# Linear attention with sparse experts on one core: first loads, last tile and last expert step rearranged

## The chip, the cores and the metric

One of the eight cores of a Trainium2 chip runs the whole program. The metric is device microseconds of one execution, the median over repeated runs. TensorE (PE) multiplies, VectorE (DVE), ScalarE (ACT) and GpSimd (POOL) do the elementwise work, and SyncE (SP) issues nearly all transfers and the transposes of activations. Each engine takes its instructions in the order in which the program lists them; an instruction that waits for a semaphore holds everything behind it on the same engine.

## The reference

Two layers, each of an attention part (A) and an expert part (B), on x of 2048 rows by 512, in bf16:

```python
def _A_ref(x, wqkv, wo):                       # x: layer-normed
    qkv = (x @ wqkv) -> q, k, v                # 32 heads of 16
    pq, pk = phi(q), phi(k)                    # phi(t) = where(t > 0, t + 1, exp(t)) + 1e-6
    kv  = einsum("bhsd,bhse->bhde", pk, v);  z = pk summed over s
    o   = (pq @ kv) / (pq . z + 1e-6)
    return o @ wo
def _B_ref(x, w_r, w_gate, w_up, w_down):      # x: layer-normed
    r   = x @ w_r
    idx = the two rows with the largest r
    y   = (silu(x[idx] @ w_gate) * (x[idx] @ w_up)) @ w_down * sigmoid(r[idx])
    return x + (y added to rows idx, zero elsewhere)
x = x + _A_ref(_layernorm(x), ...); x = x + _B_ref(_layernorm(x), ...)    # twice
```

The expert part touches two rows only, but it needs the two largest router values over all 2048 rows first.

## The kernel before, in words

The 2048 rows are 16 tiles of 128. Weights and all activations stay in SBUF. One call of `linear_attention_moe` lays down some 950 operations through `op` (lines 61 to 85): engine, estimated duration, what is read and written, PSUM or SBUF slots. `Plan.order` (115 to 171) then picks, step by step, the operation that can start first by those estimates; ties go by a due time to which `WEIGHTS` (54) adds a hand-tuned offset per kind of operation (such as 'phi_raw0') or per operation number. The result is a fixed instruction list for each engine. Nothing is rearranged at run time, so both the weights and the estimates decide what stands behind what.

**First layer, front.** `dma`, `x_load` and `xt_load` (228 to 257) load x by tiles, a transposed copy xt of the first twelve tiles (so that their keys need no transpose on the chip), and the weights. Both halves of wk go through ScalarE's queue, all others through SyncE's; every row of xt is brought in pieces of 256 elements, 512 bytes. Meanwhile PE spins on zeros (`spin`, 838, ten products). `wk_center` (857) subtracts the column mean from the key weights (wkc, two halves on DVE), `row_sums` (847) gives the row means of tiles 0 and 1 (nmr). `K_raw` (448) multiplies xt by wk for tiles 0 and 1, with a correction by a rank-one product of nmr and nwb, and by wkc for tiles 2 to 11; `phi_raw` (424) turns this into pk, two ACT operations and two of DVE (em, pk). `pre` (874) takes statistics of x on DVE (358), the scale on ACT (`rstd`, 370), the normalised tile xn on the engine that KIND1 (870) names, and its transpose through SyncE's queue (`trans`, 400). `G` (470) accumulates xn^T pk over all tiles in four PSUM banks. After the sixteen transposes SyncE issues the loads of wv, wot, wo, wd and wgu; `center` (790) needs wv.

**Rest of layer one.** `Q` (481), `kv` (501), `kw_one` (558), `den` (575) and `O` (609) give the queries, the folded weights KW, the denominators and the update of x. `mid_chain` (730) normalises the new x for the expert part and for layer two at once; K and G of layer two run while the expert step of layer one (1078 to 1206) goes on as a serial chain of small operations. Its result is patched into layer two's sums (1223 to 1300) before layer two's `kv`.

**Layer two, end.** `O(1, t)` writes the last x. The last tile is split into columns 0 to 256, 256 to 384 and 384 to 512 (623), all three in one PSUM bank; DVE adds each part, ACT squares it. `lin` (678) gives the router values. `topk` (970) is run on tiles 0 to 11 early and on all later; `gather_rows` (1379) selects the chosen rows by products with a one-hot column. Then come `gate_up` (1053), SiLU, the up product, and the down product with the direct term (1474 to 1486), the copy yo (1494) and the transfer of the two rows (1498). Beside this, `last_out` (1328) writes the other rows: OUTK (1345) names the engine of each tile, OUTG (1346) an event after which it may run, `store` (1341) sends four tiles at a time. The transfer of the two rows waits for all four stores, since it overwrites rows of them. ACT loads another function table (1447) before the last SiLU, after its outputs.

## Time and profile before

| | |
|---|---|
| median of 9 runs | 158.44 us (157.97 to 158.88) |
| profiled execution | 158.34 us, span of the trace 156.5 us, granted clock 0.995 |
| PE products | 146.5 us busy, 94% of the span |
| DVE, ACT, POOL | 130.0, 111.8, 28.3 us busy |
| PE's share of the chain that ended last | 76%; DVE 9%, ACT 6% |
| transfers | 17.15 MB, of 24499 packets 17952 under 512 B |

The busy time of PE holds modelled ends of pipelined products; twenty-two of its products (the spin and the filler L1396) compute nothing. A line of the timeline has start, length, engine, line, operation, output and inputs, and in brackets the idle time before it with what ended it. The view by stretch has, after the length, the busy us of PE, PEld, DVE, ACT and POOL, then the granted clock, the share of the transfer engines and GB/s. A line of SyncE's waits has the total, the number and the longest.

### The profile page before, as it was taken

What the parts mean: (1) busy time and instruction counts of PE and PEld (TensorE: products, weight loads), DVE (VectorE), ACT (ScalarE), POOL (GpSimd) and SP (SyncE); (2) the same over time, 40 slices, a digit from 0 to 9 for tenths busy, and PEclk for the clock granted to TensorE, in tenths of its full rate; (3) what the DMA queues carried; (4) which work ended last, traced back from release to release, by engine and by line L of the source; (5) the groups of instructions that cost most, each with busy time, mean ns of one, the idle gap of its engine ahead of it and who ended that gap; (6) DMA issues with size and microseconds to landing.
All of it is one profiled execution on the core that took longest, in us unless ns stands there. A gap on an engine that the chain in (4) does not pass through costs nothing.

```text
span 156.5 us, 3882 instructions
## 1 busy us (share of the span) xinstructions
PE 146.5 (94%) x1360; PEld 74.4 (48%) x1380; DVE 130.0 (83%) x481; ACT 111.8 (71%) x272; POOL 28.3 (18%) x78
## 2 busy tenths in 40 slices
PE   6989999998999999999999999999999999998870
PEld 2424444443544444444545545575444455465660
DVE  1799999877799999999999989843488999999840
ACT  3379899654568787799978647702478998898930
POOL 7801055200000000110321000300420000643200
PEclk9999999999999999999999999999999999999998
DMA  4999947548998000033154530000000000040560
GB/s 129 348 361 279 259 101 71 103 101 280 428 453 345 6 4 0 0 71 65 42 101 101 101 67 6 0 4 0 0 4 0 4 0 0 4 136 2 178 227 2
DMA packets 24499, 17.15 MB, mean 110 GB/s; under 512 B 17952, under 2 KB 22560, under 8 KB 24096
## 3 DMA queue, kind: packets, MB, share of 16 engines
q1 hardware_dynamic: 24184, 16.39, 36.4%
q10 hardware_dynamic: 296, 0.53, 0.9%
q8 instruction: 10, 0.16, 0.4%
q14 instruction: 9, 0.07, 0.2%
HBM read 10.62 MB, written 2.10 MB: 81 GB/s over the span
## 4 chain that ended last, share of the span: by engine, by line
PE 76%; DVE 9%; ACT 6%; issue 4%; DMA 3%; SPq 0%; ACTq 0%; DVEq 0%
PE mm L487 18%; PE g L473 17%; PE g L618 11%; PE mm L441 9%; PE mm L454 5%; DVE x L628 4%; ACT pk L1334 3%; PE tp L843 3%; DMA wv<-in_A_wv_dram 3%; DVE pq L604 2%; PE tp L581 1%; PE tp L1059 1%; PE g L563 1%; PE mm L597 1%; PE tp L711 1%
## 5 line engine op out<-in xcount | busy, mean ns | idle before, releaser
L408 ACT ACTIVATE e<-mm 128x512 bf16<-128x512 f32 x52 | 30.4, 596 | 12.6 <-PE mm L441 6.3
L473 PE MATMUL g<-pk,xn 128*128 128x512 bf16 x123 | 31.1, 379 | 0.9 <-DVE pk L432 0.6
L487 PE MATMUL mm<-xnT,wq 128*128 128x512 bf16 x121 | 31.0, 379 | 0.6 <-issue 0.3
L618 PE MATMUL g<-KW,pq 128*128 128x512 bf16 (+2 forms) x134 | 30.3, 366 | 0.6 <-DVE x L628 0.4
L636 ACT ACTIVATE sq<-x 128x512 bf16<-128x512 bf16 (+2 forms) x34 | 20.4, 601 | 2.9 <-DVE x L628 2.5
L441 PE MATMUL mm<-wk,xnT 128*128 128x512 bf16 x76 | 19.5, 379 | 0.3 <-issue 0.2
L473 PEld LDWEIGHTS <-xn 128*128 128x128 bf16 x128 | 12.0, 98 | 15.8 <-issue 2.3
L618 PEld LDWEIGHTS <-pq 128*128 128x128 bf16 x136 | 12.6, 97 | 13.9 <-issue 0.5
L412 DVE TENSOR_SCALAR em<-e 128x512 bf16<-128x512 bf16 x52 | 15.1, 297 | 3.7 <-ACT e L408 3.5
L487 PEld LDWEIGHTS <-wq 128*128 128x128 bf16 x128 | 11.4, 97 | 12.5 <-issue 0.8
L394 POOL TENSOR_SCALAR xn<-x,s,nb 128x512 bf16<-128x512 bf16 x6 | 4.9, 822 | 52.5 <-PE g L618 37.5
L419 DVE SCALAR_TENSOR_TENSOR pk<-mm,em 128x512 bf16<-128x512 f32 x20 | 13.7, 687 | 0.3
L358 DVE BATCH_NORM_STATS2 st<-x 128x6 f32<-128x512 bf16 x16 | 10.5, 673 | 3.4 <-DMA x<-in_A_x_dram 3.4
L628 DVE SCALAR_TENSOR_TENSOR x<-x,opr,g 128x512 bf16<-128x512 bf16 (+2 forms) x18 | 11.9, 683 | 0.4 <-PE g L618 0.3
L441 PEld LDWEIGHTS <-xnT 128*128 128x128 bf16 x80 | 7.4, 98 | 8.8 <-DMA xnT<-xn 0.4
L628 DVE SCALAR_TENSOR_TENSOR x<-x,g 128x512 bf16<-128x512 bf16 x16 | 10.8, 683 | 0.7 <-PE g L618 0.5
L419 DVE SCALAR_TENSOR_TENSOR pq<-mm,em 128x512 bf16<-128x512 f32 x16 | 10.7, 685 | 0.1
L411 ACT ACTIVATE rl<-mm 128x512 bf16<-128x512 f32 x16 | 9.4, 612 | 1.8 <-DVE pq L416 1.0
L604 DVE TENSOR_TENSOR pq<-pq,rd 128x1024 bf16<-128x1024 bf16 x16 | 10.4, 685 | 0.0
L454 PE MATMUL mm<-wkc,xt 128*128 128x512 bf16 x39 | 10.1, 379 | 0.1
L427 ACT ACTIVATE e<-mm,rho 128x512 bf16<-128x512 f32 x12 | 8.2, 682 | 1.2 <-PE mm L460 1.2
L373 ACT ACTIVATE lnv<-mv,eps_t 128x2 f32<-128x2 f32 (+3 forms) x18 | 5.2, 291 | 5.1 <-DVE mv L359 3.5
(263 smaller groups left out, 232.0 us busy)
## 6 DMA issues: line engine op xcount, KB each, us to landing
wgu<-in_B_wgu_dram SPq DMA_DIRECT2D x2, 1408.0 KB, 13.7
out_dram<-pk SPq DMA_DIRECT2D x4, 512.0 KB, 3.9
wd<-in_B_wd_dram SPq DMA_DIRECT2D x1, 1408.0 KB
x<-in_A_x_dram SPq DMA_DIRECT2D x4, 256.0 KB, 5.4
xt<-in_A_xt_dram SPq DMA_DIRECT2D x4, 256.0 KB, 5.5
x<-in_A_x_dram SPq DMA_DIRECT2D x2, 512.0 KB, 5.9
wk<-in_A_wk_dram ACTq DMA_DIRECT2D x2, 256.0 KB, 4.0
wq<-in_A_wq_dram SPq DMA_DIRECT2D x1, 512.0 KB, 7.3
```

The source lines that it names most:

```text
L358: dve(0.61, lambda: V.bn_stats(out=st()[:], in_=x[:, t, :]), r=[("x", t)], w=[st]).early = 4.0
L408: act(0.5, lambda: A.activation(out=e()[:], in_=p()[:], func=ACT.Exp), r=[p], w=[e], **k)
L412: dve(0.2, lambda: V.tensor_scalar(out=em()[:], in0=e()[:], scalar1=1.0, scalar2=TINY, op0=ALU.min, op1=ALU.add), r=[e], w=[em], port=True ...
L419: dve(0.6, lambda: V.scalar_tensor_tensor(out=out_ap, in0=p()[:], scalar=0.0, in1=em()[:], op0=ALU.max, op1=ALU.add), r=[p, em], w=[key], **k)
L441: T_.matmul(p()[:], lhsT=xnT[:, c, t * P : (t + 1) * P], rhs=wk[:, c, :], start=(c == 0), stop=(c == NC - 1))
L454: T_.matmul(p()[:], lhsT=xt[:, c, t * P : (t + 1) * P], rhs=w[:, c, :], start=(c == 0), stop=(t >= NM and c == NC - 1),)
L473: T_.matmul(Gs[c]()[:], lhsT=xn[:, t, gcol(c) : gcol(c) + P], rhs=pk[:, t, :], start=first, stop=last)
L487: T_.matmul(p()[:], lhsT=wq[:, i, c, :], rhs=xnT[:, i, j * D : (j + 1) * D], start=(i == 0), stop=(i == NC - 1))
L604: dve(0.6, lambda q=q: V.tensor_tensor(out=q, in0=q, in1=rd()[:].to_broadcast([P, 2, D]), op=ALU.mult), r=[rd], w=[("pq", j, c), ("pq", j, ...
L618: T_.matmul(p()[:, a : a + n], lhsT=pqt(c, t * P, P), rhs=KWs[layer][:, c, a : a + n], start=(c == 0), stop=(c == NC - 1),)
L628: dve(0.04 + 0.6 * n / D, lambda q=q, a=a, n=n: V.scalar_tensor_tensor(out=x[:, t, a : a + n], in0=x[:, t, a : a + n], scalar=1.0 if i == ...
L636: act(0.1 + 0.5 * n / D, lambda q=q, a=a, n=n, sq=sq: A.activation(out=sq()[:, 0:n], in_=x[:, t, a : a + n], func=ACT.Square, scale=float( ...
```

## The change

The first half of wk and the first x load are issued by ScalarE, the second half of wk by SyncE, ahead of its other loads. xt is laid out by pairs of tiles, so that a row of a 256-column piece is 2 KB in one stretch. The order and the earliest times of the loads change (wq behind five transposes, xt 8 to 12 ahead of them). The estimate of the transfer rate in the planner goes from 284 to 355. Weights are named by kind and number within the kind, and all are new; KIND1, MIDK, OUTK, OUTG and the starts QA, QB, QD are new too, so the order of every engine's list changes. The three parts of the last tile each have a PSUM bank. The last gather goes to two banks, two column blocks each, and DVE adds each half by itself. Gate and up start with a product by zeros that clears their banks, in three banks (gate, first four and last seven blocks of up), and add first the two column blocks of the first gathered half, then the other two. Sigmoid of the router value is made with Exp before the table load instead of Tanh after it. The down products stand in two groups (blocks 0 to 3, 4 to 10). The twelve 512-wide fillers become 24 of 128.

```diff
-    WEIGHTS = {'phi_raw0': -3.7, 'kw_one0': 3.8, ...
+    WEIGHTS = {'phi_raw0': -8, 'den1': -8, 'mid_chain0': -7.8, ...
...
+        i = self.num[self.kind] = self.num.get(self.kind, -1) + 1
+        wt = self.WEIGHTS.get(self.kind, 0.0) + self.WEIGHTS.get(f"{self.kind}#{i}", 0.0)
...
-                bw = max(bw, o.done) + o.kb / 284.0
-                o.done = bw
+                bw = max(bw, o.done - 0.4) + o.kb / 355.0
+                o.done = bw + 0.8
...
-    xt = big.tile([P, NC, NR * P], BF16, name="xt")
+    xt = big.tile([P, NR // 2, NC, 2 * P], BF16, name="xt")
...
-    for k in range(0, NC, 2):
-        dma(wk[:, k : k + 2, :], A_wk[:, k : k + 2, :], [("wk", k)], 256, eng="ACT")
+    wk_load(0, eng="ACT", prio=-50.0)
+    x_load(0, 2, eng="ACT", prio=-49.0)
     op("ACT", 1.28, lambda: nc.scalar.preload_act_table_set("natural_log_exp_and_others"), w=["table"])
...
+    wk_load(2, prio=-50.0)
+    loads = [
+        (xt_load, 0, 2, 0.0), (x_load, 2, 4, 0.0), (xt_load, 2, 4, 0.0), (x_load, 4, 6, 0.0), (xt_load, 4, 6, 0.0),
+        (x_load, 6, 8, 3.5), (xt_load, 6, 8, 3.5), (x_load, 8, 12, 5.5),
+    ]
...
-    KIND1 = ['POOL', 'DVE', 'DVE', 'POOL', 'ACT', 'DVE', 'DVE', 'POOL', 'POOL', 'POOL', 'DVE', 'DVE', 'POOL', 'ACT', 'POOL', 'ACT']
-    QA, QT = 3, 8
+    KIND1 = ['POOL', 'ACT', 'POOL', 'DVE', 'DVE', 'ACT', 'POOL', 'DVE', 'POOL', 'DVE', 'DVE', 'POOL', 'POOL', 'POOL', 'DVE', 'DVE']
+    QA, QT = 4, 6
...
-    GL = 3
+    GL = 2
...
-    QB = max(14, QA + 2)
+    QB = max(13, QA + 2)
...
-    QD = 13
+    QD = 15
...
-        parts = [(i, a, b - a) for i, (a, b) in enumerate(zip(cuts, cuts[1:]))]
+        parts = [(i, a, b - a, ps("g")) for i, (a, b) in enumerate(zip(cuts, cuts[1:]))]
...
-    OUTK = ['POOL', 'ACT', 'POOL', 'POOL', 'ACT', 'ACT', 'DVE', 'DVE', 'DVE', 'DVE', 'POOL', 'ACT', 'ACT', 'ACT', 'POOL', 'ACT']
-    OUTG = [0, 3, 0, 2, 1, 0, 2, 2, 3, 2, 1, 3]
+    OUTK = ['POOL', 'POOL', 'ACT', 'ACT', 'DVE', 'DVE', 'ACT', 'ACT', 'ACT', 'ACT', 'DVE', 'DVE', 'POOL', 'POOL', 'ACT', 'ACT']
+    OUTG = [2, 0, 1, 0, 1, 0, 0, 0, 2, 4, 3, 0]
...
-    xge, xg2 = ps("tp", [P, NC, 2]), ps("tp", [P, NC, 2])
+    xge, xg2 = ps("tp", [P, NC, 2]), [ps("mm", [P, 2, 2]) for _ in range(2)]
...
-        pe(MM, lambda: T_.matmul(sp_()[:], lhsT=warm[:, 0:P], rhs=warm[:], start=True, stop=True), r=["Odone"], w=[sp_])
+        pe(0.11, lambda: [
+            T_.matmul(sp_()[:], lhsT=warm[:, 0:P], rhs=warm[:, 0:P], start=True, stop=True) for _ in range(2)
+        ], r=["Odone"], w=[sp_])
...
-    gu2 = [ps("g", [P, NF, 32]) for _ in range(2)]
-    gate_up([(p, lambda q, p=p: p()[:, q, :]) for p in gu2], lambda c: xs2[:, c, :], "xs2", 11)
+    UH = 4
+    gu2 = [ps("g", [P, NF, 32]) for _ in range(3)]
+    for p, i, qs in zip(gu2, (0, 1, 1), (range(NF), range(UH), range(UH, NF))):
...
+        for h in range(2):
+            def f(p=p, i=i, qs=qs, h=h):
+                for c in (2 * h, 2 * h + 1):
+                    for q in qs:
+                        T_.matmul(p()[:, q, :], lhsT=wgu[:, i, c, q, :], rhs=xs2[:, c, :], start=False, stop=(c == NC - 1 and q == qs[-1]))
...
+    act(0.2, lambda: A.activation(out=th[:], in_=rv2[:], func=ACT.Exp, scale=-1.0), r=["rv"], w=["th"])
...
-    act(0.2, lambda: A.activation(out=th[:], in_=rv2[:], func=ACT.Tanh, scale=0.5), r=["rv", "table"], w=["th"])
...
-    tiny([
-        lambda: V.tensor_tensor(out=u2[:], in0=gu2[1]()[:, :, 0:2], in1=ua[:], op=ALU.mult),
-        lambda: V.tensor_tensor(out=h2[:, :, 0:2], in0=u2[:], in1=ub[:], op=ALU.add),
-    ], r=[gu2[1], "ua", "ub"], w=["h2"], dur=0.1)
+    for h, qs in enumerate((slice(0, UH), slice(UH, NF))):
+        tiny([
+            lambda h=h, qs=qs: V.tensor_tensor(out=u2[:, qs, :], in0=gu2[1 + h]()[:, qs, 0:2], in1=ua[:, qs, :], op=ALU.mult),
+            lambda qs=qs: V.tensor_tensor(out=h2[:, qs, 0:2], in0=u2[:, qs, :], in1=ub[:, qs, :], op=ALU.add),
+        ], r=[gu2[1 + h], "ua", "ub"], w=[("h2", h)], dur=0.1)
...
-        "A_xt": inputs["A_x"].reshape(S, NC, P)[: NR * P].transpose(2, 1, 0),
+        "A_xt": inputs["A_x"].reshape(S, NC, P)[: NR * P].transpose(2, 1, 0).reshape(P, NC, NR // 2, 2 * P).transpose(0, 2, 1, 3),
```

## The prediction

> **What bounds the kernel now.** I read the page's busy shares first, then busy time by stretch, then the chain of waits, then the timelines of the first 22 us and the last 18 us.

> ```profile
> PE 146.5 (94%) x1360; PEld 74.4 (48%) x1380; DVE 130.0 (83%) x481; ACT 111.8 (71%) x272; POOL 28.3 (18%) x78
> ...
> PEclk9999999999999999999999999999999999999998
> ```
> ```profile
> 12.00:16.00 4.00, 3.95 (x19) 1.86 (x19) 4.00 (x15) 3.94 (x9) 0.77 (x1) 1.00 1.28 284
> 16.00:20.00 4.00, 4.00 (x21) 1.77 (x19) 4.00 (x14) 3.48 (x9) 0.67 (x1) 1.00 0.88 238
> 30.00:40.00 10.00, 9.24 (x43) 4.13 (x43) 7.01 (x15) 4.70 (x8) 0.00 (x0) 1.00 0.66 198
> 130.00:140.00 10.00, 9.79 (x92) 5.15 (x94) 10.00 (x39) 8.51 (x28) 3.78 (x9) 1.00 0.13 42
> ```
> After each stretch's length come the busy us of PE, PEld, DVE, ACT and POOL. The middle is full: PE is idle for 1.4 us in all between 40 and 140 (the stretches 40 to 45, 45 to 60, then to 80, 100, 110, 120, 130 and 140 leave 0.05, 0.31, 0.21, 0.16, 0.15, 0.11, 0.21 and 0.21). DVE is full from 12 to 20 and again from 130 to 140. So what can move is the front (PE's useful work starts at 5.3 and has holes up to 12), one hole at 38, and the end after 141. The chain of waits agrees: it enters DVE from 127.7 to 142.5 and walks through ACT's outputs and table load afterwards. The front, from the timeline:
> ```profile
> 1.25 4.06 PE L843 MATMUL tp<-warm 128*128 128x512 bf16 x10 [1.25 <-DVE warm L260]
> 4.62 1.29 DVE L358 BATCH_NORM_STATS2 st<-x 128x6 f32<-128x512 bf16 x2 [3.12 <-DMA x<-in_A_x_dram]
> 8.21 1.28 DVE L866 TENSOR_TENSOR wkc<-wk,nwb 128x1024 bf16<-128x1024 bf16 x2
> 11.33 0.41 DVE L432 TENSOR_TENSOR pk<-rl,em 128x512 bf16<-128x512 bf16 x1
> 11.79 1.02 PE L473 MATMUL g<-pk,xn 128*128 128x512 bf16 x4 [0.60 <-DVE pk L432]
> 38.56 0.38 PE L792 MATMUL tp<-wv,elast 128*128 128x512 bf16 x1 [0.71 <-DMA wv<-in_A_wv_dram]
> ```
> PE spins until 5.31; x arrives at 4.6; the centred key weights are ready only at 9.49; the first G product waits for DVE; later PE waits 0.71 us for wv. The end, timeline and SyncE's waits:
> ```profile
> 141.54 0.38 PE L618 MATMUL g<-KW,pq 128*128 128x128 bf16 x4 [0.40 <-DVE x L628]
> 148.46 1.28 ACT L1447 ACT_TABLE_LOAD   x1
> 149.93 0.22 ACT L1461 ACTIVATE s<-s 128x22 f32<-128x22 f32 x1
> 152.55 0.29 PE L1482 MATMUL g<-wd,h 128*32 128x128 bf16 x8 [0.64 <-issue]
> 152.89 0.29 DVE L1494 CAST yo<-g 128x128 bf16<-128x128 f32 x1 [1.73 <-PE g L1482]
> ```
> ```profile
> SPq L1498 <- DMA out_dram<-pk: 2.8, 1, 2.8
> ```
> The last row transfer is held by two things that end together: the copy of yo (152.89 + 0.29 = 153.18) and the last bulk store, whose sixteenth completion is at 153.21 in the trace (the other fifteen are in by 151.71).

> **The change, part by part.** A unit is four 512-wide products, 0.86 us by its spacing in the chain.

> Loads. In the trace's completion events the medians of the first loads are x0 4.21, wk0 4.38, wk2 5.08, xt0 5.93, x2 6.63, xt2 7.46, x4 8.19, xt4 9.03. An x load (2 KB a row) adds 0.70 to 0.73, an xt load (512 B pieces) 0.83 to 0.85, the last completion comes some 0.4 later. The new order is wk0, wk2, then x0 (second on ScalarE's queue) and xt0, x2, x4, xt2, xt4: about 4.4 for wk, 4.4 + 2 x 0.71 = 5.8 for x0 and xt0 (last 6.1), xt2 7.9 (last 8.5). Earlier weights gain nothing: they are complete at 5.38 today, and the ten spin products, unchanged, end at 5.31. The x0 tile is 1.5 us later (4.59 to 6.1). 2 KB pieces are worth 0.12 each, taken in. [...]

> Front. In the built program DVE now runs statistics 0 and 1 (6.1 to 7.4), the row-sum copy (nmr, to 7.95), both wkc halves (to 9.35; 9.49 today), statistics 2 and 3 (10.7), then em, pk. The blockmask copy (0.66) has left this queue for after the K products, the norm of tile 1 for ACT, and nwb goes ahead of the first scales on ACT: the first normalised tile is ready near 9.5 instead of 7.95. PE runs K_raw 0, rank one (8.05, waits for nmr), K_raw 1, rank one, K_raw 2 to 4 (9.4 to 12.0), G0, G1. By DVE's spacing (statistics 0.64, em 0.24, pk 0.37, norm 0.36) pk0 is at 11.45, pk1 12.7, pk2 15.05. So G1 ends at 13.7 with seven units done, where today it is 14.54: 0.84 gained; then G2 waits 0.5 for pk2, and at unit 21 I have 26.3 against 26.63. Gain 0.33.

> wv. All sixteen transposes still stand ahead of wv on SyncE's queue (x 12 to 16 and wq are now between them in place of xt 8 to 12 and x 12 to 16, 0.6 us of issue each; the list ends 34.45 today). The centring product stood behind 34 units; now it stands behind 36 and the mask product. 26.3 + 15 x 0.863 + 0.1 = 39.35, when wv has landed (38.52 today): the 0.71 wait goes. Unit 36 ends at 40.66 today: gain so far 40.66 - (39.35 + 0.38) = 0.93. DVE's moved blockmask copy and one more norm in each layer (0.36 each) fall into the 3.0 us that DVE idles from 30 to 40; without that cover they cost 1.4.

> Body, 40 to 141. New weights change the whole order, but the counts do not move: between the first top-k and the second layer's patch 13 units stand in both programs, and after the last KW copy DVE has the same 4 em, 5 pq, 8 denominators' scalings and 18 x updates. I take 0; below, all 1.4 us of PE's idle time goes; above, as much is added.

> End. The last tile's three parts in banks of their own: the 0.40 wait of L618 on DVE's reader goes, but DVE works through the updates (0.74, 0.34, 0.48, 0.34) almost without a hole (0.32). The square root of the last row comes 0.2 earlier, no more, since one ACT output (0.80) still stands ahead of it. From there ACT holds five outputs (3.62), then the small Exp that replaces Tanh, the table (1.28), then SiLU: its sum is unchanged, so SiLU moves by 0.2 only, whatever the halved gather and gate save. Behind SiLU one of DVE's links goes (0.24): 0.4 earlier in all for h. Both halves of u2 precede the first half of h on DVE, so halving the down products gains nothing there. The 0.64 us of issue inside the down products follow a 16 KB instruction packet that the trace shows at 150.17, among the stores; PE has 30 rows more, so that this point falls 15 products earlier: between a gain of 0.64 (loaded in time) and a loss of 0.5 (15 products by 0.036 after the same instant). But the store ends as late: its tile 13 on POOL now waits for the second half of the gather (148.0 + 0.79 = 148.8; issued at 148.51 today), while the stores ahead of it may leave 0.25 earlier. End: between -0.6 and +0.4; I take -0.25, nearest to the stores, which hold it in both.

> Sum against the profiled run, whose own time is 158.34 (span 156.5): 158.34 - 0.93 - 0.25 = 157.16; that run is 0.10 under the median of nine, 158.44, so 157.3 for the median.

> **The rivals.**
> - More: the new order also removes body waits (up to 1.4) and the end gives its 0.6: 158.44 - 0.93 - 1.4 - 0.6 = 155.5. For it: DVE's 3.0 us of slack is filled sooner, since six Q units instead of four precede wv. Against: PE is 98% busy there, and each wait has its own cause. About 155.9.
> - Nothing: the front's gain is taken back at G's waits for pk, or the transposes run later and wv is waited for again. wv then lands at 39.4 or later. 158.4.
> - Slower: x0 lands late. nmr and wkc stand behind statistics 0 and 1 in DVE's queue, so every us that x0 is later than 6.1 delays rank one, wkc and all pk by as much, in a stretch where DVE has no slack. Issue to landing of x loads reaches 6.3 in the DMA view; 1.27 + 6.3 = 7.6 costs 1.5: 157.3 + 1.5 = 158.8, and 159.5 if the transposes follow and wv with them. It decides from 7.5 on. Against it: the bytes ahead of x0 are only wk's.
> - Clock: twelve 512-wide filler products become 24 of 128. The granted clock falls to 0.50 at 154.98, 2.1 us after the last product; the longest hole that I see in the new end is 1.0 us (after the second top-k, where three fillers stand today, 146.2 to 147.0). If it fell before the last gather, products of 4.9 us (0.61, 0.55, 0.46, 2.35, 0.98) would take twice that: about 162. [...]

> **How the numbers follow.** Forecast 0.50 (own range 156.5 to 157.9), more 0.17, nothing 0.10, slower 0.19, clock 0.04. A measurement of this kernel tells some 0.2% (0.32 us) from no change. Faster 0.67, same 0.10, slower 0.23. Low end 155.5, the bounds of the first rival; high end 159.5, that of the slow one; the clock case stays out.

> **What would show it.** Right: x statistics starting near 6, K_raw running from 9.4 to 12, no wait of the centring product, the end 0.2 to 0.3 shorter after the last x update, SyncE still waiting for a store. Wrong: statistics after 7, G waiting over 1 us in all, centring waiting again, new PE idle time over 1 us between 40 and 141, or a clock under 1.00 before 150.

## The result, and the profile after

The changed kernel takes 159.44 us (median of 21 runs, 158.45 to 162.43) against 158.40 for the kernel before (63 runs): 1.0061 times, interval 1.0042 to 1.0079. It is slower by 0.6%, where I had said 157.3 us and faster. The ratio leaves out executions that lie more than 1.5% above the fastest of their kernel, which here are those in which the clock fell for longest.

The profiled execution took 158.87 us (span 157.2), against 158.34 (156.5) before. Between those two executions the time went as follows (us, from the timelines; the first three rows are starts, the last two are ends; the last x update is L632 after, L628 before):

| milestone | before | after | difference |
|---|---|---|---|
| first statistics of x | 4.62 | 6.76 | +2.14 |
| centring of wv | 38.56 | 40.10 | +1.54, two units of 0.863 more stand ahead of it: -0.18 |
| product with ohm (L1102, L1106) | 99.47 | 100.03 | +0.56 |
| last update of x | 142.82 | 143.96 | +1.14 |
| copy of yo ends | 153.18 | 153.95 | +0.77 |

So the front gained 0.18 instead of 0.93, the body lost 1.3 instead of 0, and the end gained 0.36 instead of 0.25. (Behind yo some of the 0.77 is made up again: the two times differ by 0.53.) The page's first two parts after:

```profile
PE 148.4 (94%) x1376; PEld 75.8 (48%) x1395; DVE 132.3 (84%) x488; ACT 111.4 (71%) x272; POOL 27.4 (17%) x76
...
PEclk9999999999999999999999999999999999999959
```

PE is 1.9 us busier with 16 more products (records can be missing), and one slice near the end has half the clock. By stretch (length, then busy us of PE, PEld, DVE, ACT, POOL, then the granted clock, the transfer engines' share and GB/s):

```profile
12.00:16.00 4.00, 3.95 (x19) 1.76 (x18) 4.00 (x14) 3.71 (x10) 0.77 (x1) 1.00 0.69 154
16.00:20.00 4.00, 4.00 (x21) 1.81 (x19) 3.44 (x15) 4.00 (x10) 0.00 (x0) 1.00 0.98 187
30.00:40.00 10.00, 9.79 (x45) 4.05 (x44) 8.20 (x20) 5.29 (x9) 1.21 (x4) 1.00 0.61 168
130.00:140.00 10.00, 9.79 (x100) 5.14 (x100) 10.00 (x42) 8.54 (x26) 3.07 (x6) 1.00 0.04 13
146.00:150.00 4.00, 2.67 (x60) 2.12 (x57) 3.37 (x22) 3.98 (x8) 1.52 (x2) 0.98 0.60 200
150.00:153.30 3.30, 3.19 (x118) 2.96 (x119) 2.07 (x18) 1.14 (x2) 0.00 (x0) 0.50 0.70 239
```

PE's hole between 30 and 40 is gone (9.24 before, 9.79 after). The hole is now in 146 to 150 (2.67 busy, 3.67 before), and the stretch behind it runs at 0.50. The timeline after, front and body:

```profile
6.76 1.29 DVE L364 BATCH_NORM_STATS2 st<-x 128x6 f32<-128x512 bf16 x2 [5.27 <-DMA x<-in_A_x_dram]
8.64 0.39 PE L466 MATMUL mm<-nwb,nmr 128*128 128x512 bf16 x1 [0.32 <-ACT lnv L379]
9.94 2.32 PE L460 MATMUL mm<-wkc,xt 128*128 128x512 bf16 x10
32.90 1.04 PE L447 MATMUL mm<-wk,xnT 128*128 128x512 bf16 x4 [0.16 <-DMA xnT<-xn]
40.10 0.38 PE L796 MATMUL tp<-wv,elast 128*128 128x512 bf16 x1
79.21 1.04 PE L447 MATMUL mm<-wk,xnT 128*128 128x512 bf16 x4 [0.35 <-DMA xnT<-xn]
101.16 2.35 PE L1063 MATMUL tp<-xs,wgu 128*128 128x3 bf16 x88
```

and the end, from the same view and from SyncE's waits:

```profile
147.16 1.52 POOL L1341 TENSOR_SCALAR pk<-x,opr,nb 128x512 bf16<-128x512 bf16 x2 [2.99 <-DVE nb L1328]
148.10 0.59 DVE L1378 TENSOR_TENSOR s<-keys,s 128x8 bf16<-128x8 f32 x1
148.75 0.54 PE L1386 MATMUL mm<-s,x 128*128 128x2 bf16 x16 [1.27 <-DVE s L1378]
149.59 2.49 PE L1440 MATMUL g<-xs,wgu 128*128 128x32 bf16 x88
152.43 1.18 PE L1511 MATMUL g<-wd,h 128*32 128x128 bf16 x44
153.66 0.29 DVE L1523 CAST yo<-g 128x128 bf16<-128x128 f32 x1 [1.16 <-PE g L1511]
```
```profile
SPq L1527 <- DMA out_dram<-pk: 1.5, 1, 1.5
SPq L1527 <- DVE yo L1523: 0.9, 1, 0.9
```

Three things are to be seen. x0 is in at 6.74 and not at 6.1, and the statistics start later by that. No wait for wv stands before the centring any more. At the end the comparison L1378, 0.17 before, takes 0.59 beside POOL's output of tiles 12 and 13; PE waits 1.27 for it; and from 149.86 to 153.28 the granted clock is 0.50. SyncE waits 1.5 for the stores (2.8 before) and then 0.9 for yo, so the stores no longer hold the end.

| kernel, stretch from | share | granted in the next stretch |
|---|---|---|
| after, 146.45 | 0.16 | 0.50 |
| e2_port, 146.55 | 0.27 | 0.50 |
| b_f128, 141.88 | 0.29 | 0.50 |
| a_noT, 99.97 | 0.33 | 0.50 |
| e1_fill, 100.89 | 0.37 | 0.50 |
| before, 100.36 | 0.33 | 1.00 |
| g16, 146.84 | 0.32 | 1.00 |
| a_noT, 147.75 | 0.36 | 1.00 |

In these traces a stretch under 0.3 was followed by half the clock, and one above 0.37, run at full clock, never was; between, both are seen. What a float32 record should count is a choice of mine, which no run settles: counted twice, the first three rows become 0.25, 0.34 and 0.36, the last two 0.39 and 0.45, and both outcomes are seen from 0.33 to 0.37 only. Two places come so low: the end, where half the filler columns and the wait for L1378 leave 0.16, and the 88 gate and up products of layer one, L1063, three columns wide. Of 23 executions of after, 13 have a mean clock of 0.985 to 0.989, which is one stretch at half (median 158.85 us), six 0.976 to 0.978 (159.5 to 160.9) and four 0.964 or 0.965 (161.3 to 162.4). The records by stretch are there for profiled executions only; that the further lost stretches lie behind L1063 follows from the times, from the first experiment and from g16. A mean clock by itself does not tell where a stretch was lost: of 122 executions of before, 30 have 0.980 to 0.989 and are hardly longer (median 158.44 against 158.34 for the others), and its profiled one, at 0.995, lost the clock only from 154.98 on, after the last product.

### The profile page after: what moved, and what is told of

It is laid out like the page before. It is cut to its first block, busy times and chain, and to the rows that moved or that the text cites. A ratio compares the mean times of both kernels' runs of the same rounds, so it can differ in the third digit from the quotient of the medians.

```text
span 157.2 us, 3913 instructions
## 1 busy us (share of the span) xinstructions
PE 148.4 (94%) x1376; PEld 75.8 (48%) x1395; DVE 132.3 (84%) x488; ACT 111.4 (71%) x272; POOL 27.4 (17%) x76
## 4 chain that ended last, share of the span: by engine, by line
PE 49%; DVE 19%; DMA 6%; issue 3%; ACT 2%; POOL 1%; SPq 0%; DVEq 0%
PE mm L493 12%; PE g L622 9%; PE mm L447 8%; PE g L479 7%; DMA xnT<-xn 6%; DVE x L632 6%; PE tp L587 2%; DVE pk L425 2%; DVE pq L610 2%; PE tp L1063 1%; PE g L569 1%; DVE pq L422 1%; ACT e L414 1%; PE mm L603 1%; DVE em L418 1%
## 5 line engine op out<-in xcount | busy, mean ns | idle before, releaser
L479 PE MATMUL g<-pk,xn 128*128 128x512 bf16 x123 | 31.8, 379 | 0.3
L622 PE MATMUL g<-KW,pq 128*128 128x512 bf16 (+2 forms) x132 | 29.4, 366 | 0.3 <-issue 0.2
L447 PE MATMUL mm<-wk,xnT 128*128 128x512 bf16 x77 | 19.4, 379 | 0.9 <-DMA xnT<-xn 0.5
L622 PEld LDWEIGHTS <-pq 128*128 128x128 bf16 x136 | 12.6, 98 | 13.7
L425 DVE SCALAR_TENSOR_TENSOR pk<-mm,em 128x512 bf16<-128x512 f32 x20 | 13.7, 686 | 0.2
L447 PEld LDWEIGHTS <-xnT 128*128 128x128 bf16 x80 | 7.4, 98 | 10.9 <-DMA xnT<-xn 2.6
L632 DVE SCALAR_TENSOR_TENSOR x<-x,opr,g 128x512 bf16<-128x512 bf16 (+2 forms) x18 | 12.0, 683 | 0.3 <-PE tp L587 0.3
L400 POOL TENSOR_SCALAR xn<-x,s,nb 128x512 bf16<-128x512 bf16 x5 | 3.8, 768 | 44.4 <-issue 44.4
L425 DVE SCALAR_TENSOR_TENSOR pq<-mm,em 128x512 bf16<-128x512 f32 x16 | 10.9, 685 | 0.2
L632 DVE SCALAR_TENSOR_TENSOR x<-x,g 128x512 bf16<-128x512 bf16 x16 | 10.6, 682 | 0.0
L460 PE MATMUL mm<-wkc,xt 128*128 128x512 bf16 x39 | 9.6, 379 | 0.1
L400 POOL TENSOR_SCALAR xn<-x,rho,nb 128x512 bf16<-128x512 bf16 x7 | 5.9, 846 | 16.6 <-DVE nb L387 15.6
```

The source lines that it names most:

```text
L400: e.tensor_scalar(out=xn[:, t, 0:D], in0=x[:, t, :], scalar1=s_, scalar2=b_, op0=ALU.mult, op1=ALU.add)
L425: dve(0.6, lambda: V.scalar_tensor_tensor(out=out_ap, in0=p()[:], scalar=0.0, in1=em()[:], op0=ALU.max, op1=ALU.add), r=[p, em], w=[key], **k)
L447: T_.matmul(p()[:], lhsT=xnT[:, c, t * P : (t + 1) * P], rhs=wk[:, c, :], start=(c == 0), stop=(c == NC - 1))
L479: T_.matmul(Gs[c]()[:], lhsT=xn[:, t, gcol(c) : gcol(c) + P], rhs=pk[:, t, :], start=first, stop=last)
L622: T_.matmul(p()[:, 0:n], lhsT=pqt(c, t * P, P), rhs=KWs[layer][:, c, a : a + n], start=(c == 0), stop=(c == NC - 1),)
L632: dve(0.04 + 0.6 * n / D, lambda p=p, q=q, a=a, n=n: V.scalar_tensor_tensor(out=x[:, t, a : a + n], in0=x[:, t, a : a + n], scalar=1.0 if ...
```

## The experiments

Times are medians; ratios are to the kernel before on the same chip in the same session (its medians 158.24 to 158.42). My theory at the start was that the clock at the end ate the gain, and with it L1378, which took 0.59 us beside POOL's output; the rivals were the loads and the body's order. All fillers and widened columns below compute nothing that is used.

**e1_fill: the end's hole filled.** Four 512-wide products go ahead of the last gather, into its bank.

```diff
-        pe(0.22, lambda h=h: gather_rows(xg2[h], eqL, lo, lo + 4, [2 * h, 2 * h + 1]),
+        pe(0.22, lambda h=h: ([T_.matmul(xg2[0]()[:], lhsT=warm[:, 0:P], rhs=warm[:], start=True, stop=True) for _ in range(0 if h else 4)],
+                              gather_rows(xg2[h], eqL, lo, lo + 4, [2 * h, 2 * h + 1])),
```

> The changed kernel, with four 512-wide filler products on TensorE between the transposes of the second top-k and the last gather (where the changed kernel's trace shows TensorE without work from 147.47 to 148.75); nothing else moves, and the fillers compute nothing. Theory 'clock' (the hole is what drops the granted clock to 0.50 from 149.9 on): the clock stays at 1.00 until after the down products, gate and up take about 2.35 us instead of 2.49 and the 44 down products about 0.98 instead of 1.18, so some 0.3 us less, a median near 159.1, and no executions of 160 and more with a mean clock under 0.98. Rival 'the clock falls for another reason' (the sum of work in the tail, or a fixed place): the drop stays where it is, median 159.4, spread unchanged. Rival 'the fillers delay the gather': 0.1 to 0.3 us more.

159.09 us, 0.9996 (0.9957 to 1.0034). The drop at the end is gone: from the last x update to the end of yo it takes 9.58 us against 10.00. Seven of twelve executions had a mean clock of 0.997 or more (157.06 to 159.32, median 158.33), five 0.977 to 0.988 (159.8 to 161.24). The profiled one is of the latter, and shows where:

```profile
100.00:104.00 4.00, 3.96 (x104) 3.00 (x103) 2.11 (x13) 0.00 (x0) 0.00 (x0) 1.00 0.00 0
104.00:107.00 3.00, 3.00 (x44) 1.71 (x42) 1.56 (x7) 2.00 (x5) 0.00 (x0) 0.55 0.03 5
107.00:111.00 4.00, 4.00 (x25) 1.70 (x22) 1.79 (x10) 0.94 (x4) 0.00 (x0) 0.50 0.00 0
```

PE counts as busy throughout (3.96 of 4.00), and the clock halves all the same, behind L1063. So the end's drop costs about 0.4 us, and there is a second drop in the body, in some executions only.

**e2_port: POOL off the path.** The output of tile 12 goes from POOL to DVE.

```diff
-    OUTK = ['POOL', 'POOL', 'ACT', 'ACT', 'DVE', 'DVE', 'ACT', 'ACT', 'ACT', 'ACT', 'DVE', 'DVE', 'POOL', 'POOL', 'ACT', 'ACT']
+    OUTK = ['POOL', 'POOL', 'ACT', 'ACT', 'DVE', 'DVE', 'ACT', 'ACT', 'ACT', 'ACT', 'DVE', 'DVE', 'DVE', 'POOL', 'ACT', 'ACT']
```

> The changed kernel, with the output of tile 12 on VectorE instead of GpSimd: one instruction leaves GpSimd's list and stands in VectorE's list right behind nb (L1328), all other lists are the same. Theory 'port' (the one-hot step L1378 that took 0.59 us instead of 0.17 was held by GpSimd's second output, 147.92 to 148.68): L1378 takes 0.17 us again, the last gather starts 0.42 us earlier, the copy of yo with it; the stores end about 0.85 us ahead of yo in the changed kernel, so they allow it. Median near 159.0. The hole of TensorE ahead of the gather shrinks from 1.28 to 0.86 us; if the granted clock then stays at 1.00, 0.3 more, 158.7. Rival 'the 0.42 us are not on the path': 159.4. Rival 'VectorE has no room for it': the output's 0.41 us delays MAX8 (L987) by up to that much, and the gain is gone, 159.4.

159.97 us, 1.0010 (0.9977 to 1.0044).

```profile
147.70 0.16 DVE L1378 TENSOR_TENSOR s<-keys,s 128x8 bf16<-128x8 f32 x1
```

The 0.42 us in L1378 goes, but the end is no shorter (9.96): the clock stays at 0.50 for longer there, and the 44 down products take 1.37 us instead of 1.18. The two causes cover each other.

**a_noL: xt in 512 B pieces again.**

```diff
-    xt = big.tile([P, NR // 2, NC, 2 * P], BF16, name="xt")
+    xt = big.tile([P, NC, NR * P], BF16, name="xt")
```

> The changed kernel with the transposed x in DRAM in its old layout, so that each row comes in 512-byte pieces again; SBUF layout, order of the loads and every engine's list are unchanged. Theory 'the pieces matter': each of the first transposed loads lands 0.12 us later and those behind it too, 0.36 by the third; the first key products start with the column sums of the first one, so 0.1 to 0.4 us more, median 159.5 to 159.8. Rival 'hidden': nmr, the scales and the centred weights set the first key products, and the median stays at 159.4.

159.18 us, 1.0030 (0.9993 to 1.0067), with first statistics at 5.42 instead of 6.76. Its seven executions with a single drop have a median of 158.30, those of after 158.85. Taking the 2 KB pieces away is no loss; what it gains this run can't settle. Contrary to the expectation's words, the layout of xt in SBUF changes with that in DRAM.

**a_noT: the new loads and body with the old end.** Two of the lines that go back:

```diff
-    xge, xg2 = ps("tp", [P, NC, 2]), [ps("mm", [P, 2, 2]) for _ in range(2)]
+    xge, xg2 = ps("tp", [P, NC, 2]), ps("tp", [P, NC, 2])
...
-    gu2 = [ps("g", [P, NF, 32]) for _ in range(3)]
+    gu2 = [ps("g", [P, NF, 32]) for _ in range(2)]
```

> Loads, front and body of the changed kernel with the tail code of the kernel before (one bank for the last tile, whole gather, gate, up and down, Tanh, twelve 512-wide fillers, its engines and weights for the outputs). Theory 'body' (the changed kernel loses 1.1 us before the last x update and wins 0.4 behind it): the clock stays at 1.00, the last x update ends about 1 us later than in the kernel before, and the median is 159.4 to 160. Theory 'tail' (the clock and the port in the new tail are the whole loss): 158.2 to 158.5.

160.0 us, 1.0083 (1.0055 to 1.0112). Seven executions without any drop lie at 159.12 to 160.17 (median 159.68), above before's 158.24: loads and body alone cost 1.4 us. The first statistics and the centring of its profiled execution:

```profile
6.15 1.29 DVE L364 BATCH_NORM_STATS2 st<-x 128x6 f32<-128x512 bf16 x2 [4.66 <-DMA x<-in_A_x_dram]
39.31 0.38 PE L798 MATMUL tp<-wv,elast 128*128 128x512 bf16 x1
```

With the same loads as after, x0 is complete at 6.13 here and the centring starts at 39.31, about where I had forecast both (6.1 and 39.35), and the kernel is slow all the same. Three with one body drop lie at 160.88 to 161.59, two with two at 162.9 and 163.0. So the loss is not at the end; the end hides part of it. Nor is it, in this execution, in the front.

**g16: sixteen columns in layer one's gate and up.** The products of L1063 stream 16 columns instead of 3, beside e1_fill's fillers.

```diff
-    xs = big.tile([P, NC, 3], BF16, name="xs")
+    xs = big.tile([P, NC, 16], BF16, name="xs")
...
-    gu = ps("tp", [P, 2, NF, 3])
+    gu = ps("tp", [P, 2, NF, 16])
```

> The changed kernel with the four fillers of e1_fill ahead of the last gather, and with layer one's 88 gate and up products (L1063) fed 16 columns in place of 3 (columns 2 to 15 are all ones; only columns 0 to 2 are read, as before); every list stays as in e1_fill. Theory 'clock in the body': in five of twelve executions of e1_fill the granted clock fell to 0.50 for one or two windows of 3.41 us right behind these products, because they fill TensorE's columns for only a few per cent of 2.4 us; 16 columns raise the share of a window that holds them from about 0.35 to 0.48, weight loads still set their pace (2.4 us), so the clock stays up in all executions: mean clock 0.994 or more in each, none above 159.6, median 158.3 (that of the undisturbed executions of e1_fill). Rival 'the body's drop has another cause' (chip, temperature, the sum of work): again four to six of twelve with a mean clock of 0.99 or less, median near 159.

158.91 us (157.67 to 159.60), 1.0019 (0.9991 to 1.0047). The groups of L1063, after and then here (nanoseconds of one: least, median, most):

```profile
L1063 PE MATMUL tp<-xs,wgu x88: 164/164/178, 101.2 to 103.3; 128*128 128x3 bf16 x88
```
```profile
L1063 PE MATMUL tp<-xs,wgu x88: 169/169/183, 102.3 to 104.5; 128*128 128x16 bf16 x88
```

88 products take 2.36 us instead of 2.35. No execution is above 159.6, eleven of twelve have a clock of 0.993 or more: the body's drop is gone, and the 88 products cost no more. The median that I had expected, 158.3, it misses by 0.6. The drop was the slow tail of the times; the typical execution is where it was, so the clock is not the whole of the loss.

**g16p: both repairs of the end.** g16 with e2_port's change.

```diff
-    'DVE', 'DVE', 'POOL', 'POOL', 'ACT', 'ACT']
+    'DVE', 'DVE', 'DVE', 'POOL', 'ACT', 'ACT']
```

> As g16, and the output of tile 12 on VectorE as in e2_port. Theory: the three costs (clock in the tail 0.4, clock in the body, port 0.4) are separate and add up: no clock drop, L1378 at 0.17 us, the copy of yo 0.4 earlier than in g16, median 157.9, so 0.3 below the kernel before. Rival 'the stores': the last bulk store's completion, 0.5 us ahead of yo in e1_fill, becomes the end: 158.2 or more.

158.13 us, 0.9995 (0.9964 to 1.0026). With the clock held, freeing L1378 is worth 0.0024 of the time by the two ratios, or 0.4 us, though the intervals overlap. The kernel is now level with before, and the 1.2 us that I had predicted is still missing.

**f_noD: the split of the first loads undone.** g16 with both halves of wk on ScalarE's queue and x0 first on SyncE's; every engine's order is held as g16's by a list, so that the planner can't rearrange the rest.

```diff
+    ORDER = '#0 #3 #22 #1 #4 consts0#0 #2 #5 #7 #6 #8 #10 #9 consts0#1 wk_center0#0 stats0#0 ...'
...
-    x_load(0, 2, eng="ACT", prio=-49.0)
+    wk_load(2, eng="ACT", prio=-49.0)
...
-    wk_load(2, prio=-50.0)
+    x_load(0, 2, prio=-50.0)
```

> As g16, with the order of all engines written down as it was, but with the first loads as in the kernel before: both halves of wk on ScalarE's queue, x of tiles 0 and 1 first on SyncE's. Theory 'the split costs': x0 lands at 4.6 instead of 6.7, statistics and scales are ready before nmr, and the centred weights come 0.5 to 0.7 us earlier; if that lasts, the median is 0.3 to 0.7 below g16 (157.6 to 158.0). Rival 'taken back': the second layer's transposes and the expert chain, which set the pace later, are no earlier, and the median equals g16's within 0.2. Rival 'wk decides' (what the split is made for: with both halves behind each other on one queue the second lands later than the spin's end): slower than g16.

158.36 us, 0.9996 (0.9969 to 1.0023), statistics from 4.80 on. Against g16's 1.0019 that is some 0.4 us, or 0.55 by the medians. x0 is complete at 4.78, but now xt0 (5.78) is in ahead of the second half of wk, issued 0.02 us before it from the other queue and complete at 6.17 (5.38 in before). So f_noD doesn't undo the overtaking; it moves it to another load.

**g16L: the 2 KB pieces undone,** in g16.

```diff
-        dma(xt[:, a:b], A_xt[:, a:b], [("xt", t) for t in range(lo, hi)], 128 * (hi - lo), after, **k)
+        dma(xt[:, :, lo * P : hi * P], A_xt[:, :, lo * P : hi * P], [("xt", t) for t in range(lo, hi)], 128 * (hi - lo), after, **k)
```

> As g16, with xt in DRAM in its old layout (512-byte pieces), every list unchanged; the test of a_noL without its clock drops. Theory 'the pieces matter': 0.1 to 0.4 us above g16 (158.91), 159.0 to 159.3. Rival 'hidden' (statistics, nmr and the centred weights set the first key products, not xt): 158.9 within 0.2. a_noL against the changed kernel speaks for hidden.

157.86 us, 0.9977 (0.9946 to 1.0008): 0.4% under g16. Statistics start at 5.34 instead of 6.86.

**g16x: the overtaking undone alone.** g16 keeps the 2 KB pieces and the split wk; only x0 goes behind wk2 on SyncE's queue, ahead of xt0. The order is held.

```diff
-    x_load(0, 2, eng="ACT", prio=-49.0)
+    x_load(0, 2, prio=-49.0)
```

> As g16, with 2 KB pieces and the split weights kept, but x of tiles 0 and 1 behind wk's second half on SyncE's queue, ahead of xt0, instead of behind wk's first half on ScalarE's; nothing else moves. Theory 'overtaking' (with 2 KB pieces xt0 is issued in 0.41 us instead of 0.68, so that it runs beside x0 from the other queue, and x0's last completion goes from 5.3 to 6.7): x0 is complete near 5.3 again, the statistics start there, and the median is 0.5 to 0.9 below g16 (158.0 to 158.4), as in g16L. Rival 'piece size itself' (the 2 KB pieces cost something else than x0's arrival): as g16, 158.9.

157.75 us, 0.9964 (0.9938 to 0.9991): 0.55% under g16 (the two intervals meet at 0.9991), and faster than before. The first statistics of g16x and of g16L, and the centring of g16 and of g16x:

```profile
5.22 1.29 DVE L312 BATCH_NORM_STATS2 st<-x 128x6 f32<-128x512 bf16 x2 [3.73 <-DMA x<-in_A_x_dram]
```
```profile
5.34 1.29 DVE L363 BATCH_NORM_STATS2 st<-x 128x6 f32<-128x512 bf16 x2 [3.84 <-DMA x<-in_A_x_dram]
```
```profile
40.42 0.38 PE L796 MATMUL tp<-wv,elast 128*128 128x512 bf16 x1
```
```profile
39.06 0.38 PE L744 MATMUL tp<-wv,elast 128*128 128x512 bf16 x1
```

The centring is 1.36 us earlier, and PE no longer waits for a transposed tile ahead of it. This is the cause in the front of after and g16. The completions of the transfers (us, issue and then first to last of sixteen) show how:

| | before | after | g16x |
|---|---|---|---|
| x0 | 0.80, 3.94 to 4.59 | 1.26, 5.67 to 6.74 | 1.28, 4.87 to 5.20 |
| xt0 | 1.28, 5.75 to 6.21 | 1.28, 5.00 to 5.93 | 1.73, 5.53 to 5.85 |
| x2 | 2.00, 6.43 to 7.25 | 1.73, 6.73 to 7.63 | 2.21, 6.31 to 8.09 |
| time to issue xt0 | 0.674 | 0.407 | 0.432 |

In after x0 is issued 0.02 us ahead of xt0, from the other queue, and xt0 is in 0.8 us before it. The 2 KB pieces are issued in 0.41 us instead of 0.67, which is what brings xt0 level with x0; SyncE's next load follows at 1.73. With x0 ahead of xt0 on one queue it is in at 5.20. How much x0 loses differs between executions with these same loads: it is complete at 6.74 in after, 6.76 in g16p and 6.84 in g16, but at 6.13 in a_noT, 6.15 in e2_port and 6.23 in e1_fill. xt0 is ahead in all six.

**b_split: the split alone, in the kernel before.** x0 second on ScalarE's queue, the second half of wk first on SyncE's, 512 B pieces, order held.

```diff
-        dma(wk[:, k : k + 2, :], A_wk[:, k : k + 2, :], [("wk", k)], 256, eng="ACT")
+        dma(wk[:, k : k + 2, :], A_wk[:, k : k + 2, :], [("wk", k)], 256, eng="SP" if k else "ACT")
...
-        load(lo, hi, after, prio=-50.0 + i)
+        load(lo, hi, after, prio=-50.0 + i, **({} if i else {"eng": "ACT"}))
```

> The kernel before, its order written down, with x of tiles 0 and 1 second on ScalarE's queue and the second half of wk first on SyncE's; every other load and every list unchanged. Theory 'the split costs': x0 lands at 6.7 instead of 4.6, and the statistics, which stand first on VectorE, hold the blockmask copy, nmr and the centred weights behind them: 1.0 to 2.0 us late at the first key product with wkc, of which the wait for wv (0.71) takes in some: 159.0 to 160. Rival 'hidden': 158.4. Rival 'earlier weights gain': below 158.2.

159.44 us, 1.0054 (1.0029 to 1.0078). Here x0 isn't overtaken (5.40, xt0 6.21), and yet the split costs 0.9 us: x0 is 0.8 later than in before, and x2's last piece comes at 8.45 instead of 7.25. So in before's order the split costs by itself. In the changed order the 2 KB pieces add to it (g16 against g16L); what the split alone costs there no run shows, and g16L, which has it, is no slower than before.

**b_f128: the narrow fillers alone, in the kernel before.** Twelve fillers of 512 columns become 24 of 128, order held.

```diff
-        pe(MM, lambda: T_.matmul(sp_()[:], lhsT=warm[:, 0:P], rhs=warm[:], start=True, stop=True), r=["Odone"], w=[sp_])
+        pe(MM, lambda: [T_.matmul(sp_()[:, 0:P], lhsT=warm[:, 0:P], rhs=warm[:, 0:P], start=True, stop=True) for _ in range(2)], r=["Odone"], w=[sp_])
```

> The kernel before, its order written down, with each of its twelve 512-wide fillers made two of 128 columns; nothing else. Theory 'fillers' (the narrow fillers alone drop the clock in the tail): windows of the tail fall below a third of TensorE's columns, the granted clock drops to 0.50 ahead of the gate, up or down products, a mean clock of 0.985 to 0.99 with 0.2 to 0.5 us more, 158.6 to 158.9. Rival 'place' (it is the hole of 1.28 us ahead of the last gather, where the changed kernel has no filler at all; in the kernel before the hole is 0.57): clock and time unchanged, 158.3 to 158.4.

157.94 us, 0.9977 (0.9958 to 0.9996). My expectation of a loss missed.

```profile
145.00:152.00 7.00, 6.63 (x149) 5.91 (x149) 5.12 (x34) 5.37 (x9) 0.79 (x1) 0.52 0.68 226
152.00:155.00 3.00, 0.80 (x44) 0.63 (x44) 0.29 (x1) 0.00 (x0) 0.00 (x0) 0.98 0.03 9
```

The clock falls in eleven of twelve executions (0.968 to 0.986), in the profiled one from 145.3 to 152.1, and the time does not suffer: half clock beside ACT's outputs costs nothing there, and it is back for the down products, which run as 44 in 0.86 us without the 0.64 us of issue that before has between its 36 and 8. What a dropped stretch costs depends on what PE does in it.

**f_body and f_mv2: the order of DVE in the body.** f_body is f_noD with two steps of the list moved: near 74 us a normalised tile (xn, L400) goes ahead of a key step (pk, L425), so that its transpose starts earlier; near 98 us another key step goes behind the small steps that make the expert's factor sg (L1130 in after). f_mv2 moves only the second.

```diff
-    G1#0 phi0#65 phi0#66 norm0#21 K0#7
+    G1#0 phi0#66 norm0#21 phi0#65 K0#7
...
-    mid#10 phi1#8 phi1#33 picks0#1
+    mid#10 phi1#33 picks0#1
...
-    patch#6 mid#11 mid#6
+    patch#6 mid#11 phi1#8 mid#6
```

> As f_noD, with two steps of VectorE's list moved by a few places and nothing else: the normalised tile (L400, 74.6 in g16p's trace) ahead of the pk step (L425, 0.6 us) that stands before it, and another pk step (97.8) behind L1130 instead of ahead of L1007, L1008, L1051 and the copy L1257. Theory 'waits of the body are order': the transpose that holds K of layer two at 78.8 (wait 0.35 to 0.4) starts 0.6 earlier, and the products L1106 of the expert chain stop waiting 0.23 and 0.07, so 0.4 to 0.6 less than f_noD (158.36): 157.8 to 158.0. Rival 'each wait has another behind it': same as f_noD within 0.2. Rival 'pk becomes late': G or Q waits for it, slower than f_noD.

> As f_noD with the second of f_body's two moves alone (pk of 97.8 behind L1130; the normalised tile stays behind its pk step). Theory 'two separate waits': half of what f_body wins, 0.2 to 0.6 below f_noD's 158.36, so 157.8 to 158.1, and f_body's 157.05 needs both. Rival 'the expert chain alone': the same as f_body, 157.1. Rival 'the transpose alone': the same as f_noD, 158.3.

f_body: 157.05 us, 0.9925 (0.9901 to 0.9949; seven runs, 156.99 to 157.89). f_mv2: 158.33 us, 0.9995 (0.9964 to 1.0027), the same as f_noD. So the normalised tile, or it together with the key step, is worth 1.1 to 1.3 us. PE's timeline at that place, in f_noD and then in f_body (L395 is after's L447):

```profile
74.22 1.02 PE L395 MATMUL mm<-wk,xnT 128*128 128x512 bf16 x4
79.02 1.04 PE L395 MATMUL mm<-wk,xnT 128*128 128x512 bf16 x4 [0.78 <-DMA xnT<-xn]
```
```profile
74.86 1.02 PE L395 MATMUL mm<-wk,xnT 128*128 128x512 bf16 x4 [0.40 <-DVE pk L373]
78.71 1.03 PE L395 MATMUL mm<-wk,xnT 128*128 128x512 bf16 x4
```

The wait of 0.78 for the transposed tile (0.35 in after, at 79.21) goes, and half of it comes back as a wait for pk. That is 0.4 us net, and the two profiled executions differ by 0.1 (157.97 and 157.89, the latter the slowest of its seven); where the rest of the medians' gain sits the traces don't show.

**f_best: everything together.** f_body with 512 B pieces and DVE for tile 12, its output one place earlier in the list.

```diff
-    xt = big.tile([P, NR // 2, NC, 2 * P], BF16, name="xt")
+    xt = big.tile([P, NC, NR * P], BF16, name="xt")
...
-    'DVE', 'DVE', 'POOL', 'POOL', 'ACT', 'ACT']
+    'DVE', 'DVE', 'DVE', 'POOL', 'ACT', 'ACT']
```

> The changed kernel with all that the runs blame undone at once and the rest of the change kept: x0 first on SyncE and both halves of wk on ScalarE's queue, 512-byte pieces, the two moves of f_body, the output of tile 12 on VectorE, four fillers ahead of the last gather, 16 columns in layer one's gate and up. Theory 'the change's gains are there and were covered by these costs': f_body's 157.05 less 0.4 for the port and 0 to 0.4 for the layout, 156.3 to 156.7, as good as the kernel before with the new tail (156.77). Rival 'one cover, several names' (each of them moves the same wait): no better than f_body, 157.0.

157.59 us, 0.9955 (0.9936 to 0.9974), not better than f_body alone. The costs do not add up; that they are partly one slack counted under several names is my reading. The trace offers one place for it: the end is 0.17 us shorter than in f_body (9.40 against 9.57), but the last store is now complete at 152.38, 0.05 us ahead of the end of yo's copy (0.76 in f_body), so that an earlier yo would gain nothing more.

**b_new: the old loads and body with the new end.** The kernel before, its order held, with the end of the changed kernel, the four fillers, DVE for tile 12 and 16 columns.

```diff
-    xge, xg2 = ps("tp", [P, NC, 2]), ps("tp", [P, NC, 2])
+    xge, xg2 = ps("tp", [P, NC, 2]), [ps("mm") for _ in range(2)]
```

> The kernel before up to its last O products (its loads, 512-byte pieces, its order written down), then the changed kernel's tail (banks of their own, halved gather, gate, up and down, Exp in place of Tanh, its engines for the outputs) with the four fillers and the output of tile 12 on VectorE; 16 columns in layer one's gate and up. Theory 'body costs, tail wins': the last x update ends as in the kernel before (142.8), the rest takes 9.2 us in place of 10.36, a median of 157.1 to 157.3. Rival 'stores': the bulk stores end as late as before (they held the end together with yo there), 158.0 to 158.3. Rival 'the tail wins nothing by itself': 158.2 or more with yo late.

156.77 us (155.44 to 157.60, six runs), 0.9886 (0.9838 to 0.9934): faster than before by 1.1%, and than after by more. In the profiled execution, the slowest of the six:

```profile
PE tp L738 <- DMA wv<-in_A_wv_dram: 1.0, 1, 1.0
...
PE g L421 <- DVE pk L380: 0.4, 1, 0.4
```
```profile
SPq L1470 <- DMA out_dram<-pk: 1.5, 1, 1.5
```

The wait for wv, which the change was to remove, is still there with 1.0 us, and the kernel is the fastest of all. From the last x update to the end of yo it takes 9.21 us, against 10.36 before and 10.00 after. The end, with the repairs of g16p, is where the change holds its worth.

## Why the prediction was wrong

The sum was -0.93 at the front, 0 in the body, -0.25 at the end. In the profiled pair it was -0.18, +1.3, -0.36, or +0.77 at the end of yo. In the medians it is +1.04, since ten of the 23 executions also lose the clock in the body. Two steps failed: the body taken as 0, and the landing of x0 with the front's gain behind it. The first failed in every profiled execution with these lists, the second in after, g16 and g16p.

- **"4.4 + 2 x 0.71 = 5.8 for x0 and xt0 (last 6.1)" failed.** x0 lands at 6.74. The sum counts bytes, as if the two loads shared evenly and neither came first; the order of arrival is what counted. "2 KB pieces are worth 0.12 each, taken in" had the right sign by itself (from x2 on, x loads and xt loads now arrive 0.65 to 0.70 apart, xt 0.83 to 0.85 before), but their quicker issue brought xt0 ahead of x0. g16x prices that alone at 0.55% (0.9 us), as much as the front's missing gain of 0.75. In a_noT, e2_port and e1_fill x0 came at 6.13 to 6.23, though behind xt0, and the centring at 39.31 to 39.64: there most of the front's gain was made. It did not help: in e2_port the last x update ends at 143.59, 0.77 later than before, so the body lost 1.5 there.
- **The slow rival had one mechanism right, and its range (158.8 to 159.5) holds the median partly by luck.** It was "x0 lands late", deciding from 7.5 on, and against it I held that only wk's bytes stand ahead of x0. xt0's stood there too. It priced x0 alone; that 6.76 was enough is due to the body's loss, which no rival held. b_split, slower by 0.5%, shows that in its order the split costs by itself.
- **"At unit 21 I have 26.3" came out by luck:** 26.43, with x0 0.6 later than the sum had it. Where x0 landed as forecast (a_noT), unit 21 ends at 25.82, so the sum from x0 to there was some 0.5 too long and the late x0 made up for it.
- **"26.3 + 15 x 0.863 + 0.1 = 39.35" failed.** 40.10: it assumed no wait in fifteen units. There is a wait for a transposed tile at 32.90: the four products issued at 31.71 need 0.863, so the hole is 0.33 (the profile, which models the ends, counts 0.16 as idle). The rest is lost in smaller holes. In g16x the hole is gone and the centring starts at 39.06. That the wait for wv goes was right, and did not pay.
- **"Body: I take 0; above, as much is added" failed towards its upper bound:** +1.3 of at most 1.4. Its step was that equal counts of units cost equal time. PE's waits of over 0.1 don't show the loss: 0.35 (79.21) and four of 0.11 to 0.16 after, against 0.40 (141.54) and five of 0.15 to 0.16 before. Narrow products between the centring and the last x take 19.13 us instead of 18.64, each up to the start of the next; the rest is spread. That the order on DVE makes such a difference is shown by f_body against f_noD and f_mv2; that it is the whole of the 1.3 isn't. By the same count the five profiled executions with these lists and no drop in the body (after, e2_port, a_noL, g16, g16p) lose 1.3 to 2.2, f_noD, with the old first loads, 1.5, f_body 1.0, and three with before's lists (b_f128, b_new, b_split) 0.1 to 0.6. So the loss comes with the order; which steps of it carry it stays open.
- **The clock rival, given 0.04, happened,** as far as the mean clocks tell, in all 23 executions at the end (0.4 us) and in ten of them at L1063 as well (about 1.5 us for one stretch, 2.6 for two, by the groups' medians). It was at neither place as I had put it: I looked for long holes, and PE's longest is 1.27. That holes so short cost no clock was my estimate, and e1_fill speaks against it: with that hole filled the drop at the end is gone. Ahead of the drop behind L1063 PE counts as busy for 3.96 of 4.00 us (e1_fill): it is the share of streamed columns that was low there, 0.37, and 0.16 at the end of after.
- **"End: I take -0.25" was right in size and partly by luck.** The stores, which I had as the bound, are no longer last; the 0.64 us of issue (0.4 in a_noT, 0.6 in b_split) is absent from every kernel here whose instruction queue has eleven packets instead of ten, after among them, so the better bound came true, though no run shows that the packets are the cause; the clock (0.4) and L1378 (0.42) took it back. Without these two the new end is worth 1.1% on the old loads and body (b_new, six executions; 1.15 us from the last x update to yo in its profile), well beyond my bound of -0.6.

What stays open is which of the body's many small steps carry its loss, and how the costs share one slack: taken one by one, overtaking (0.9), order (1.1 to 1.3), clock and L1378 (0.4 each at the end) and clock in the body (159.44 against 158.85, 0.6 in the median) come to more than the 2.1 us between forecast and median, and f_best shows that they do not add.

## What to carry to other kernels

When a first-needed tile is moved to a second queue, compare what the first queue issues in the same microsecond: quicker issue there can bring another load ahead of it (here xt0, issued in 0.41 us instead of 0.67, was in 0.8 us ahead of x0). Count TensorE's streamed columns, not its busy time: here stretches of 3.413 us with a share of 0.16 to 0.29 were followed by half the clock, and of those with 0.32 to 0.37 some were. Where the share comes so low, try a wider moving operand (3 to 16 columns cost 0.01 us for 88 products, and in g16 eleven of twelve executions had a clock of 0.993 or more). And when a planner rearranges everything, judge the parts with the rest of the order held: here the new end, with its repairs, was worth over 1%, and the new loads and order hid it.

## What the runs showed that I had not expected

- In these traces the clock changes at the ends of equal stretches of 3.413 us whose start differs from execution to execution, and goes with the columns streamed in the stretch before (0.16 to 0.29: half the clock); a kernel whose share is 0.33 to 0.37 at one place drops in some executions and not in others (a_noT, e1_fill: five of twelve each). Half clock can be free (b_f128: 0.52 from 145 to 152, and 157.94 us).
- Three small DVE steps took 0.5 to 0.59 us instead of 0.16 while POOL worked on 512 columns: L1378 in after, and there too L1007 and L1008 (0.50 at 98.54 and 0.51 at 99.08) beside POOL's L1094 (98.41, 1.16 us). In before the same two steps (97.69 and 97.88) took 0.16 each, and POOL's copy starts behind them, at 98.16. In e2_port, with POOL's output of tile 12 moved to DVE, L1378 took 0.16. What holds them no run shows. Not every step is held: L1415 took 0.20 in after (147.98), in the same stretch of POOL's work.
- Two loads issued 0.02 us apart from two queues arrived in the other order, 0.8 us apart.
